# A new order of TensorE's groups and new offsets for the other engines' work, in a kernel that two long strings schedule

## The chip, the cores and the metric

The kernel runs on one core of one Trainium2 chip. The core has a matrix engine (TensorE, PE in the profile, with PEld for its weight loads), a vector engine (VectorE, DVE), an activation engine (ScalarE, ACT), GpSimd (POOL) and SyncE (SP), which here only issues DMAs. Each engine works through its own queue in order, and queues wait for each other through semaphores. The metric is the device time of one execution in microseconds, as a median of several.

## The reference, cut to what matters

Four blocks in a row, each added to a residual stream `x` of 2048 tokens by 448 features: attention with a recurrent memory, a gated feed-forward, and the same two with the same weights again.

```python
def _A_ref(x, mem0, Wq, Wk, Wv, Wo, seg_len):      # 16 heads of 256, 8 memory rows, segments of 32
    mem = mem0
    for s in range(n_seg):                          # 64 segments
        h = concat([mem, x[segment s]])             # 40 rows
        q, k, v = h @ Wq, h @ Wk, h @ Wv            # per head
        p = softmax(where(mask, q @ k.T * scale, -1e9))
        o = sum over heads of (p @ v) @ Wo
        mem = o[:8]                                 # goes into the next segment
        outs.append(o[8:])
    return concat(outs)

def _B_ref(x, W_gate, W_up, W_down):
    return (relu(x @ W_gate) * (x @ W_up)) @ W_down

x = x + _A_ref(layernorm(x), ...);  x = x + _B_ref(layernorm(x), ...)
x = x + _A_ref(layernorm(x), ...);  x = x + _B_ref(layernorm(x), ...)
```

The memory makes each attention block a chain of 64 segments that can't be worked on side by side. The token rows of a segment and the feed-forward can be done at leisure once their memory or their `x` is there.

## The kernel before, in words

**Weights.** In the first part of the run Wq, Wk, Wv and Wo come in by DMA; TensorE transposes them (L750) and multiplies them to per-head products `A` (Wq times Wk) and `Bsb` (Wv times Wo) (L763), which ScalarE and VectorE copy out of PSUM. From then on attention needs only `A` and `Bsb`.

**The chain.** `chain(step)` (from L907) does the memory rows of both attention layers together, the second seven steps behind the first (`LAG = 7`), so there are 70 steps. A step is a row of six hops between TensorE groups. U: two groups of 56 matmuls multiply the memory by `A` (L936), and VectorE turns the result in 32x32 blocks (L1107, L1114). Scores (L1130), then a softmax on VectorE and ScalarE. P: a transpose of the probabilities (L451 with `Pm`). Y: probabilities by rows (L1187, L1190), copied to `YTm`. O: 56 matmuls with `Bsb` in groups of 20, 20 and 16 (L975), split into a high and a low part by ScalarE and VectorE (L981, L982). cols: eight small matmuls (L451 with `Sel`) that turn the result into columns, copied to `mT` (L998), which the next step's U reads. In some steps more rows ride in the spare columns of these groups (the functions `ride` and `third`; tiles `Pr`, `PTr`, `Tr`).

**The rest.** `att_group` does the token rows of a tile of 128 tokens (L1276 for U, L1302 scores, L451 for the output), `glu_units` and `glu_down` the feed-forward (L1374, L1379, L1380, L451), `norm` a layer norm with its transposes. `tiles` adds these beside the chain's steps.

**The order.** Nothing is issued as it is written. Each operation is entered by `_Sched.add` with engines that may do it, a cost in ns, what it reads and writes, and a priority. `_Sched.schedule` then plays all engines against these costs and puts out one list for each engine.

- TensorE's list isn't chosen by priority. `line` (L189 on) takes the 2179 TensorE groups in the order in which the program enters them, and each letter of the string `LINE` (L46 on) says which of those that are left comes next: A is the first that is left, B the second, and so on; `~` adds 80. A group may be some few matmuls or 56.
- On the other four engines the plan takes, whenever one is free, the operation with the lowest priority among those ready. Chain operations have level 0 and go first. All else has `now`, the chain step that it belongs to, plus an offset from the string `ORDER` (L33 on): each letter is the offset of one unit of work (such as one weight load, one layer norm, one feed-forward quarter), from -6.5 to +6.5 steps in quarters. Work that either ScalarE or VectorE may do goes to the one that is free first in the plan.
- Where the plan sees TensorE idle for more than about 300 ns, `filler` puts in matmuls that compute nothing (L1408), for four fifths of the hole. A change of the tile shape of TensorE (`mode`: the whole array, 32 columns, 64 rows and so on) costs the plan `TURN = 94.0` ns.
- `emit` writes the lists out with semaphore waits, and ScalarE begins with a table load (L401).

```python
    def line(self):
        left = [o for o in self.ops if "pe" in o.engs]
        ...
            out.append(left.pop(k + SIGNS.index(c)))
    def part(self):
        self.unit += 1
        self.shift = 0.25 * (STEPS.index(ORDER[self.unit]) - 26) if self.unit < len(ORDER) else 0.0
    def add(...):
        ...
        o.prio = ((self.now if now is None else now) + (self.shift if level > 0 else 0.0), level)
```

Of the kernel before, what the change touches and what calls it, by code (L numbers as in the profile page):

```python
# [12 lines left out]
D = 448  # L13
H = 16
# [15 lines left out]


STEPS = "ABCDEFGHIJKLMNOPQRSTUVWXYZabcdefghijklmnopqrstuvwxyz0"
ORDER = ("WaAPMPvTtHAmiKXsPbQwBZAAKVLahkUWfxoglheAggVZZIjCfbeJAXlzkAApmXXSQGGARFrGGMUgYLYEqpMcimntsnbaLdDaYNUaIKQasootaa"  # L33
         "IamHzatMbanGYaAKt0aaJQPfHNWZggWPXLeJgyAiS0Lu0paxXy0bJaaawJabqAwkXQsLnJ0P0xdYLuR0IrxJESoh0aprYvAKeakBaTde0apmfl"
         "0AxKjloNZCHdAbpsDsUzAeRDrSYQfCauramiRROdJWQSliYOAntmwDkLvpaU0ose0NVHbcTnnAxX00lknAmXoAEI0JXsWoNrWtaR0aBTzbAueA"
         "zxZcQ0q0gag0TH0DuL0awknFmlrwNUBkrnZMushahJaOgAABbmsGORqpMzXeAbTAdCgmAA0qpoI0a00TKDzwtajkhAYHgKXubMoLxaAcZMeAky"
         "UPvecasMa0GlwBpnnaDqvPuaft0lUJZwIPBAtdSRexIzd0gdp0TFG0ZVaWtamLdLF0tecZgoaFmCnSxLrSAKbVEWWUbAUcbZAQKUWznAD0DwFY"
         "LhfiQS0H0vSOAAXZbJUSsFaria0uvIkcEZwBqzeVgvNgOaALCXLR0bnstXIDN0xuLBcRcqpzdacfaiZlTMhk0gMMHRwaBkgAisGZYtMsUFn0zV"
         "IFNwJApRZfcAiutYgwLmYo0w0xvGkIAceuiXs0DasLaajayO0oeyil0F0AqRaRioYDVAtQYbmvOVuSte0WMUqA0yKPaKRav0IjNTTO0lKZJvdk"
         "PxyqdoWnhLpAGweRybtOxXTBtFxgRZFGuwtA0XA0luZtjAvlcgOC0JAfaBWaBpTiUEtfuUcpuev0O0plQOMQhQAShmmAGTYotfgpbleII0TaBM"  # L40
         "aPnZY0dxoBWpVcrAiqamnnNot0unVPyLvpKpqAsABVrANdQWsSSKlz0JcSfj0ElEpn0qPKwWzaAgaYo00Aa0Tlb0oupJCA0yVSxuTnA0zokfbp"
         "CrqRqZjtboAdaHNayVAlkpQAMirRvHYYjqcposgwBwuwNAPImgFcnygdasArDIapCO00J0IZchpGLumthtqLsYG0apAkaPAtIR0rAB0uPdaaaa"
         "aacpbuKLoaaaaaaaaaaaaaaaaaaaOmqe0NbraUgWsbrP")

SIGNS = "ABCDEFGHIJKLMNOPQRSTUVWXYZabcdefghijklmnopqrstuvwxyz0123456789+-*/=<>()[]{}.,:;!"
LINE = ("AFFFEIFLJHFEFEFEJJEFGFHEEAEDMHHEDDEDEDDLKHDGDFDDDDKAJ,CEDEDCCCCKJAEGCEDBBMBBIACEBDCAAJALAHEnAADCCFGDEBAdcAWAMA"  # L46
        "AWnBAETkCSBBAHANNAgMBAKBWCAHAHGBbDAUDCAYBHBAAADPAENREAFLQHABQFPPFAFBDACCCCFBBABAAAWAAAKARBAHOdAGSAZAQAAABMS~DB"
        "A~BggA(AeCAAbAa9AZZZDADCAETADDQQAAAAMAAKKKAJJAIHAHGABEBACABAAAABATMAXAKVcLKAMRX~JXAMLA~NAAAEEADGAaaFFCCABETBBR"
        "WACPAANNNOAALAMvLA0DJCIHHLGGGGAFHHAADEKAACBBAEAAAABAMBAYXQAJGaIIAQAVAAAGDDAODDdcAFBBDDAAUaAACRAQBBNNNNAALAALL3"
        "3JKArIOICHBGGGAFIHeAEAEAACBBFAAAABCAATMBAXWeAJUaKJhMAW]AcKKAAAKEEATDA76fGmF2CABF4yBxAAAuuuCBbsAEpRFponEAAAjBLB"  # L50
        "glQAe9eeeECHcbTcbSBYBuFWBAATAARAJDSOOOAAMANLNMBdAbJDIAAPGUGZBgYBeEEEFHAGQDAvuCD~LCCqADAnNrm~BDCkkkFAAhDD;hhAAA"
        "cdjDACCYAAAVaAUATTTA0TBRDQQBBANAAAKCJBAHHHAKHGBBSGGAdcDEAZALQCBKZJBXBBBUIcJIFFBADGA))CEEon/H)CAB9jA7KD5556AA3H"
        "A32Ahzhy4FAAvAulCsssAiBEEonBFmmlDDATNCflCWABbJJEYsYYYCYXKXAWWAAITAAAAPODVNbNNNAALLEJAK+9YYDD5AA9E2FA0DIyyyzAOH"
        "vAvvBRsRBxqADACCAAjDAhDCFieeeAAcDJAaaxCCAXAAVAZAnSSssWARRRBABANAAZAACBAAGYSdlSSHGhZAFRAVAMDYABBeKBBBxHYBJEEB)("
        "HGDACOG+CA=B7ADe4CAG1112bAAyAAxxwdDkAzsbBFgoEnEmmmneFAEiENihFf-DeAGchABa2IZZZBCXAYIVXWEATDARCAAOfTBNUBMMMPBLEA"
        "L98DXeDVGIA0FAQAwFDTt~JDssstAZApArqDnANDCjAiEAmAfCCdAcccEAAZAYAAAWWAAAaTSvnARsRABBANNNAAMLAAXdAAAqBTGdASFFhPYF"
        "AQAACSBBgMBBBbIBQEBI{]ACSCC<FECCA+LEA7gD5556AA3A44bAiz70AZAxAwvluuuvAcsGHqqqGGAFtmFFFjIiBEAEeeeINEeAaAcbFBkEYA"
        "GATaAASRDHPVDOOOAANMA//ACIJA8=OOVH4Nc26BA000BAPyDwAvvNCSCAqEBAnNClCoAjjjEAiAgOC4CeeAAAbCAYBBAVqyVAAASSSASoACAA"
        "AMAAKYAdtkCJVIATISAGZgAFAAACNARMBeLdBBBFQFBADA))FCEoE/CAN>BE8B7AnCC333AGA0A21EYEexvAAVtb;rriBBArnnnCDmlQAkkPCB"
        "NAmfAAAcAaaBZZZCAYXFXHWWIAGADRXAAPANNEMMMEMVVNLEJRA77Ife4AHA16B0BAyyyAfCAuAtvuAsKAJpDAtHmAlBBKiiiEAAfAeCBddEAA"  # L60
        "DCXAWAAUZAAmStSSSASogAAAOBibxAvAZAAjYXgAJeYViYJJBnAASGAAARDC1cCJAZIBBBzIyIBEJEEBD77GFAnCIC0AB4BxB~NwAXuuu~GDtA"
        "VAtsGFADoAPsAljAjiANMfffAAdNAAdcBQYZAOBJUBLSBWRrGQQQRSDIDNDGNMLAFaJCAAGOATAEYEEEIFAACAAxwCMCTsABDBHnsAmMCBjjjA"
        "JAhCfAgfC}BAcDAAZYBXAAVVVWAATAVUsrSTAYuBRAAOOAAMMMAAKAYeAtkBWJBAIHkRbRFGSBdBEUEDOAMCCCGGCFIC{]ItU,(ADAA/BA-NB9"
        "99+AKA6CA65CdBA81bAAA3x3BwvmuuuActtsGtsHGGzpGGGmGApkjISAAfffEDdOcIeee;DaHbDYDejYfPWWeWWWXAAUNBBcbB/xQQYAdDAVDM"
        "TCARRRAACRPOKQQDGLCAAKIAAHAFFAEEEAACCABAWOVJHMARXFBAUAHAAGFAAALCCPDCDCFAJJFEBBBBBAABAADAAAAABAAAAA")


class _Op:
# [19 lines left out]
class _Sched:  # L88
# [29 lines left out]
# [5 lines that stand above are left out]
# [66 lines left out]
    def line(self):  # L189
# [3 lines left out]
        k = 0  # L193
        for c in LINE:
            if c == "~":
# [1337 lines left out]
```

## Time and profile before

| what | value |
|---|---|
| time, median of three runs | 1505.74 us (1505.22 to 1508.84) |
| time of the profiled execution | 1504.3 us |
| its span, first to last instruction | 1501.8 us |
| PE busy | 1487.6 us, 99% of the span, 37022 matmuls |
| PEld busy | 1057.6 us, 70% |
| DVE, ACT, POOL busy | 1148.6, 908.3, 171.8 us (76%, 60%, 11%) |
| granted TensorE clock | 1.000 |
| DMA | 34.11 MB; 228 and 186 GB/s in the first two of 40 slices (75 us), 4 to 65 GB/s after them |

Busy time on PE counts a matmul from its start to its modelled end. Matmuls follow each other before the one ahead has ended (a 128x448 one lasts 352 ns, and the next starts 189 ns after it), so short pauses don't show as idle. To see them one has to look at the starts: a group's time here is from its first matmul's start to the next group's first start.

### The profile page before, as it was taken

What the parts mean: (1) busy time and instruction counts of PE and PEld (TensorE: products, weight loads), DVE (VectorE), ACT (ScalarE), POOL (GpSimd) and SP (SyncE); (2) the same over time, 40 slices, a digit from 0 to 9 for tenths busy, and PEclk for the clock granted to TensorE, in tenths of its full rate; (3) what the DMA queues carried; (4) which work ended last, traced back from release to release, by engine and by line L of the source; (5) the groups of instructions that cost most, each with busy time, mean ns of one, the idle gap of its engine ahead of it and who ended that gap; (6) DMA issues with size and microseconds to landing.
All of it is one profiled execution on the core that took longest, in us unless ns stands there. A gap on an engine that the chain in (4) does not pass through costs nothing.

```text
span 1501.8 us, 83238 instructions
## 1 busy us (share of the span) xinstructions
PE 1487.6 (99%) x37022; PEld 1057.6 (70%) x37022; DVE 1148.6 (76%) x3561; ACT 908.3 (60%) x2519; POOL 171.8 (11%) x664
## 2 busy tenths in 40 slices
PE   9999999999999999999999999999999999999999
PEld 6557666667767776777768677677768776677776
DVE  6667678787778878687877877687777788787864
ACT  7776566666556666566655666466665556565643
POOL 3110111111111111011100111011100011010000
PEclk9999999999999999999999999999999999999999
DMA  7612100000000000000000000000000000000000
GB/s 228 186 31 65 50 11 8 12 9 8 8 4 16 8 8 14 4 18 6 16 5 11 12 8 15 4 17 6 18 4 8 13 9 14 5 11 5 12 8 11
DMA packets 62581, 34.11 MB, mean 23 GB/s; under 512 B 31872, under 2 KB 62096, under 8 KB 62224
## 3 DMA queue, kind: packets, MB, share of 16 engines
q1 hardware_dynamic: 62224, 28.80, 7.5%
q8 instruction: 291, 4.77, 1.3%
q14 instruction: 66, 0.54, 0.1%
HBM read 21.36 MB, written 1.84 MB: 15 GB/s over the span
## 4 chain that ended last, share of the span: by engine, by line
PE 95%; DVE 3%; ACT 1%; SPq 0%; issue 0%; DMA 0%; POOL 0%; DVEq 0%
PE psG L451 24%; PE psG L1276 17%; PE psG L1374 12%; PE psC L975 11%; PE psC L936 9%; PE psG L936 3%; PE psG L1187 3%; PE psG L763 3%; PE psG L1302 3%; PE psC L451 2%; PE psC L1187 1%; PE psC L1130 1%; PE psG L750 1%; PE psG L1190 1%; PE psC L1276 1%; PE psG L975 1%
## 5 line engine op out<-in xcount | busy, mean ns | idle before, releaser
L1276 PE MATMUL psG<-HT,A 64*128 64x128 bf16 x4968 | 285.7, 216 | 0.2
L451 PE MATMUL psG<-Bsb,YT 128*128 128x448 bf16 x1288 | 276.6, 352 | 0.0
L1276 PE MATMUL psG<-HX,A 64*128 64x128 bf16 x3726 | 266.9, 216 | 0.2 <-issue 0.2
L1276 PEld LDWEIGHTS psG<-HT,A 64*128 64x128 bf16 x4968 | 234.2, 94 | 13.7 <-issue 5.4
L441 ACT ACTIVATE Ug<-psG 64x128 bf16<-64x128 f32 (+2 forms) x428 | 153.6, 378 | 68.3 <-PE psG L1276 59.4
L1276 PEld LDWEIGHTS psG<-HX,A 64*128 64x128 bf16 x3726 | 194.0, 94 | 1.0 <-issue 0.8
L1374 PE MATMUL psG<-G,glu 64*128 64x128 bf16 x5936 | 187.9, 216 | 0.6 <-DVE G L444 0.2
L1374 PEld LDWEIGHTS psG<-G,glu 64*128 64x128 bf16 x5936 | 174.2, 94 | 12.8 <-issue 6.3
L975 PE MATMUL psC<-Bsb,YTm 128*32 128x448 bf16 x3584 | 181.4, 353 | 1.0 <-DVE YTm L444 0.6
L451 PEld LDWEIGHTS psG<-Bsb,YT 128*128 128x128 bf16 x1288 | 112.5, 97 | 89.3 <-issue 5.9
L936 PE MATMUL psC<-A,mT 64*32 64x448 bf16 x3948 | 154.7, 350 | 1.5 <-DVE Pr L1160 0.5
L1114 DVE STREAM_TRANSPOSE uT<-Usb 128x384 bf16<-128x384 bf16 x280 | 154.1, 551 | 0.9
L936 PE MATMUL psG<-A,mT 64*32 64x448 bf16 x3892 | 152.1, 350 | 0.0
L975 PEld LDWEIGHTS psC<-Bsb,YTm 128*32 128x32 bf16 x3584 | 89.9, 97 | 73.4 <-DVE YTm L444 3.1
L441 ACT ACTIVATE YT<-psG 128x448 bf16<-128x448 f32 x238 | 120.6, 543 | 11.3 <-PE psG L1190 10.4
L444 DVE CAST Ug<-psG 64x128 bf16<-64x128 f32 (+2 forms) x274 | 112.8, 422 | 18.4 <-PE psG L1276 14.6
L936 PEld LDWEIGHTS psC<-A,mT 64*32 64x32 bf16 x3948 | 79.6, 92 | 58.1 <-ACT mT L441 5.9
L1379 ACT ACTIVATE hG<-psG 128x512 bf16<-128x512 f32 (+1 forms) x126 | 68.5, 544 | 65.6 <-PE psG L1374 61.6
L451 PE MATMUL psG<-glu,hG 128*128 128x448 bf16 x448 | 98.6, 352 | 0.0
L1380 DVE TENSOR_TENSOR hG<-hG,psG 128x512 bf16<-128x512 bf16 (+1 forms) x117 | 70.7, 610 | 32.5 <-ACT hG L1379 31.5
L981 ACT ACTIVATE Ohi<-psC 128x448 bf16<-128x448 f32 x66 | 35.9, 544 | 95.5 <-PE psC L975 94.2
L936 PEld LDWEIGHTS psG<-A,mT 64*32 64x32 bf16 x3892 | 79.8, 92 | 17.3 <-ACT mT L441 0.6
(242 smaller groups left out, 2889.4 us busy)
## 6 DMA issues: line engine op xcount, KB each, us to landing
HR<-xn SPq DMA_DIRECT2D x128, 32.0 KB
Tsb<-Rsb SPq DMA_DIRECT2D x256, 1.5 KB
Tsb<-Rsb SPq DMA_DIRECT2D x256, 2.0 KB
Bsb<-in_A_Wq_dram SPq DMA_DIRECT2D x6, 384.0 KB
Bsb<-in_A_Wk_dram SPq DMA_DIRECT2D x6, 384.0 KB
HR<-Rsb SPq DMA_DIRECT2D x126, 1.5 KB
HR<-Rsb SPq DMA_DIRECT2D x126, 2.0 KB
X<-in_A_x_dram SPq DMA_DIRECT2D x16, 112.0 KB
```

The costliest lines, as they stand in the source:

```text
L441: return E.activation(out, i, ACT.Copy, scale=1.0 if scale is None else scale)
L444: return E.tensor_copy(out, i)
L451: return E.matmul(out, lhsT=lhsT, rhs=rhs, **k)
L763: i = E.matmul(bk.ap()[row0:row0 + mn, 0:D], lhsT=lhs[:, et, m0:m0 + mn], rhs=rhs[:, et, :], start=(et == 0), stop=(et == 1), tile_positio ...
L936: i = E.matmul(ub[v].ap()[32 * j:32 * j + 32, 0:D], lhsT=self.mT[rw, WHERE[b], first:first + 32], rhs=cols, start=(b == 0), stop=(b == 6), ...
L975: x = E.matmul(bo.ap()[32 * j:32 * j + 32, 0:D], lhsT=self.YTm[:, q, :], rhs=self.Bsb[:, chunks[q], :], start=(i == 0), stop=(i == 13), ti ...
L1114: self.s.add("dve", 578, lambda E, e, out=out, hh=hh: E.transpose(out, heads[hh]), r=[("Usb", 2 * half + v) for v in range(2)], w=[f"uT{ha ...
L1187: return E.matmul(ps[:, n * q:n * q + n], lhsT=HR[rows, 128 * q:128 * q + 128], rhs=PT, start=True, stop=True, tile_position=(b, 0))
L1276: i = E.matmul(ub[v].ap()[:, 128 * n:128 * n + 128], lhsT=self.A[rw, b, a0:a0 + 128], rhs=HT[rw, WHOLE[b], :, 0:SEG] if CROSS[b] is None e ...
L1374: i_ = E.matmul(two[v].ap()[:, 128 * c:128 * c + 128], lhsT=self.Wgu[rw, b, f0:f0 + 128], rhs=G[rw, WHOLE[b] if CROSS[b] is None else 4 + ...
L1379: s.add("act", 170 + 0.833 * N, lambda E, e, dst=dst, z=two[0], N=N: E.activation(dst, z.ap()[:, 0:N], ACT.Relu), r=[two[0]], w=[("hG", i, ...
L1380: s.add("dve", dv_cost(N), lambda E, e, z=two[1], N=N, dst=dst: E.tensor_tensor(dst, dst, z.ap()[:, 0:N], ALU.mult), r=[two[1]], w=[("hG", ...
```

## The change

Only two strings change, `ORDER` and `LINE`; both keep their lengths (1144 and 2188 letters). No cost, no operation, no buffer and no line of the scheduler changes. 918 of the 1144 offsets differ, by 3.7 steps in the mean over all units. TensorE's list holds the same 2179 groups: 1711 of them stand at another place, half of the 2179 by at most two places, a tenth by nine or more. Which of ScalarE and VectorE does a copy, the order of the four other queues (SP's DMA issues too) and the place and length of the fillers follow from the two strings through the plan.

```diff
-ORDER = ("WaAPMPvTtHAmiKXsPbQwBZAAKVLahkUWfxoglheAggVZZIjCfbeJAXlzkAApmXXSQGGARFrGGMUgYLYEqpMcimntsnbaLdDaYNUaIKQasootaa"
+ORDER = ("XVAPMPSPU0eQshNDJHlyQAAKEKFYTTnKhsVEoiWWUsPWZFARZjHv0fMpppVAINWUUAOrD0QTKksvPJgInbSAlblsqlxarfpaoAOa0ePaAklvaa"
...
-LINE = ("AFFFEIFLJHFEFEFEJJEFGFHEEAEDMHHEDDEDEDDLKHDGDFDDDDKAJ,CEDEDCCCCKJAEGCEDBBMBBIACEBDCAAJALAHEnAADCCFGDEBAdcAWAMA"
+LINE = ("AFEEEEIIEGFEFEADLDJDHGEEEDADCKIDDEDDECDCJJDHCABBCBCBI:JHBDBBBBCBI/HEDBFBCBCBKJHEEBBBBCJMQAIALHBABBCBAACBcbCDQA"
...
```

More of the change, by code (lines that the diff above doesn't have):

```diff
@@ L32 @@
 STEPS = "ABCDEFGHIJKLMNOPQRSTUVWXYZabcdefghijklmnopqrstuvwxyz0"
-ORDER = ("WaAPMPvTtHAmiKXsPbQwBZAAKVLahkUWfxoglheAggVZZIjCfbeJAXlzkAApmXXSQGGARFrGGMUgYLYEqpMcimntsnbaLdDaYNUaIKQasootaa"
[L34 to L43, printed above, removed]
@@ L45 @@
-SIGNS = "ABCDEFGHIJKLMNOPQRSTUVWXYZabcdefghijklmnopqrstuvwxyz0123456789+-*/=<>()[]{}.,:;!"
-LINE = ("AFFFEIFLJHFEFEFEJJEFGFHEEAEDMHHEDDEDEDDLKHDGDFDDDDKAJ,CEDEDCCCCKJAEGCEDBBMBBIACEBDCAAJALAHEnAADCCFGDEBAdcAWAMA"
[L47 to L65, printed above, removed]
@@ new lines @@
+ORDER = ("XVAPMPSPU0eQshNDJHlyQAAKEKFYTTnKhsVEoiWWUsPWZFARZjHv0fMpppVAINWUUAOrD0QTKksvPJgInbSAlblsqlxarfpaoAOa0ePaAklvaa"
+         "kaDeOadS0aKAVafat0aazKWAaNyNXfiPeVuAGylprp0uru0wsw0E0aaaGRaxybEaX0yGIn0XoMgxLwXAAcxczAOvYaEEAqASAawYaubP0apdBA"
+         "sTxVVYRNZUv0niphIsAAAexRNc0AEDanFaSSG0adAY0VWivQtAcmy0EgWp0VoIpAuNHdofTutDcgsHlQoqXfoPSQhoXVUTrEuvaboax0AKKuVn"
+         "WAncs0R0QajonAPDvHgUaAhFSLLWZUUFFdAaPGfaDNaXX0NvbFhG0iqIAqLJAlfFKXgpPcDQhkY0gmJvKgs0eAjeceOkAGAuuQvEAaVwaUJASC"
+         "moqJ0aFJaQnWiSpJynhYv0sAe00KopJkIyFurlwneQIvUVgNiFsVyPlCaLBa0nmAn0cszQVohYYJdSNCBgWKfMARARUZULd0OQCstQyAAPAPGd"
+         "kzfmqu0n0EuOViX0EvncHIaGna0fxVAc0JqxgzwNZeagVksirXHIGpAjMXFVAC0ucDpHYjs0naAwaUgBoIhILJLYH0lwAsgw0uoVYqAiGGRvOV"
+         "tsczJPYIAtcumpA000AmO0oomxGtOtmcMtXQNkAaAaauXfFS0HVf0e0rMAUXaTUj0AVjfQR000OAJua00LqkwckmjJabRaA0iHrTyIRYaZYbDC"
+         "dxAmVLdndMkAN0ADyh0HAXApAiOg0onIXR0s0AOiCIZBuAgDcCrEijEJafxagtPenEAAKbdpUXIqt0ReMAvQrmZxqYsAVWknQfjIM0kVPkbaAi"
+         "aArgBmdD0EUlVDXociaEYhTQtrwpaLMPjpHjtEsjpRdtNeUA00QuczhBsRJjjfobBnogkgx0faNeaMNuVkaAaQREoCXUHF0fviaYTDHwHGuYbA"
+         "OcRdqSykHAZVaCdaVIGhqpAdHEtRmWRNMqmAc0JwpLstiGnRmPLPAymSaZorejTAgj00VhynXhSyEcEtsLKYDJiQaXOTaqy0WB0S00fPLuaaaa"
+         "aawW0IKgJaaaaaaaaaaaaaaaaaaaJtaktN0AagUYWbrA")
@@ new lines @@
+SIGNS = "ABCDEFGHIJKLMNOPQRSTUVWXYZabcdefghijklmnopqrstuvwxyz0123456789+-*/=<>()[]{}.,:;!"
+LINE = ("AFEEEEIIEGFEFEADLDJDHGEEEDADCKIDDEDDECDCJJDHCABBCBCBI:JHBDBBBBCBI/HEDBFBCBCBKJHEEBBBBCJMQAIALHBABBCBAACBcbCDQA"
+        "BFDUAOjAAQAPDeANNAgMBAKBAAHbICGBDAZCCLAAHAVAGXAADOADMCCADPJFAHOENNEHFEBACGBBBABAAAWAAAKARBAHOdHASAZAQAAAUNB~DB"
+        "A~BggA(DACcAAaADY7EDWWWGAATADDRQAAAAMAAKKKAJJAIAIHABFAADACBAAAABAMSZhAAKVLbKASM~JXALLA~NAAAEEAHDAGFYYCHCCUABBX"
+        "RACPAANNNAALAKMvLA0KCPJIICHHHAGIIAAEFAADCCBAEAAABABAMAAXXHAOIaASIAWGAAAGDDAOACCcbBEBADCAbADSAAQAPBAMMMMAAKALL3"
+        "3LJQAqJIIBHHHAGAIHeAAFDAACBBFAAAABCAAMSBAXWeKAUaJiJAXLdAsLKAAAEEIATDAC65ElEHCAzBBx2AweDCtttGAAqAsrDPDAAmkBLBin"
+        "QAffVeeeBUDcHZZZCYYwHBFAUAAAREJADrNhDMMMNAAKAYLDIKJZIgfDHAAFTKFeFFFbBTAGDACuuD~MCCAqBPDBmAl~BCBjjjEjAAgDC:hgFd"
+        "AAbEDZAAAWbAAUAXTTTAASyAQCQPAANAAAKPAAIAHHHKAGBTBGGdAVACACLBVKKbNBRiBLVLBBBRFFBEAAF[)Gqp<CCA)*NA+MB888EKAA4A65"
+        "BjBA1zAZ4DAAvuctCjrrrArhHEFXlFmlAD7jpACYCfLCdcDbbbCJZbZAAYYBFAUUAAAAQACT5OcCCMMMPNAKKAK98ZYJ5DAAU1ABzKAxxxAxIC"
+        "uTDSCssABoAouCAlCBjADIgEDAdddAAbACbbyDCXAXAAAUAYSvSlsARRRACAAAMAAKYADjAiIaUAAlHGRhQAYFAQAACYBBfeLLBBBFKFBAUDA>"
+        ">oGFC*CCCADB6ACd3BA5111FaAAxAzynDctAtbiIBTotFnmEEkkkVkbEEgADDeeL9GDJaAiAYdXXqXXXBJVAWWoIAbUSAACQAAdCNqMSMMMPFM"
+        "rAAJAH33VUCCzAAE2PvACtTCCqqqAQBDnmAnmD]CjAiADAfCCdAgEbbbAAZAABAXXAUAAaTSvnARsRABBANNNOAALAYeAAiBqIUBAHGQiaQAFA"
+        "APACSBBgBBBJIaBEBOI]]ACCC>AQBCC(-BEA8hD666AA4A55AbA2EA6AzxXxdvdAtttICrAFrrEADmunPDDDDinQgFkfDEJcccAAaCZaZFBhXB"
+        "BAETAXDHQHDUOOOAAMA==DKAKIA8POHA4AL2R111AAPzyACyyCTCSuLFqxAApOnn~AEDlllAlAAiQDAhgD2CdAcEAgAZDCXAAAAASSSTAoSDBd"
+        "AANAAAAWjAiIUZDAGGRAAOeEAAANBRhBLVLBBBFFBEHMAA))FRFo=CCCAE9=LA7oDD444AAF1AEz10EgxYwAAAcVxriq}ApppADDmAQmmCCPjC"
+        "CCmgABcdJCCZBYYYCCXHVAVWVHAJRAAAOGTAALbLRLLLVLNKKR98AffJ4A9CkA0BByADwwwAAuuAvuBKAqJpAAnHBAk>AAiiiJDAgAeAAAddDA"
+        "ZDCXAAVAATASuSSSAShoAAAPBBMBZfvACjXABWVAdHTTaBBSGFAQZPiENWNAMNDLABBVtIBBBFnQBEGBD87EoEmAeCCAyBBDv0eAt~JDCrrr~D"
+        "VqqAgqpHnETSAjAoADgBfBeeeBBBcbMREaZCXBWObAFTFZFRGAEOOOAGAMLALLKcFaAPIAAOUGAAEXEEEAACCBCAwvCLBSAZpAICAlqBkLBiii"
+        "AJDAeAdfeC{BbAaACAXBBVAYUUUAASATTqqRARuQCPAOAAMMMAMAKAAXdtCBIUogUJIAbRFBYFRcBBDCOCALBBBFKAEADA))sGS<CAB*AB+M99"
+        "9A9DKA5A76CdBk9A1ADxAYwA01uultttAcsHqqGrqHoGfGlrAFFipFBgHfffAFedJOuecddDDI{YZDDDWbVEUdUUUACVLRAXQaZw-QEXAAVNZD"
+        "TMOCQQQFAAQNADCPOAJAAKIAAHFAEEADDDUEACAQBAITAbAZAFXJENJDHAABHADDAPCCACBLADACCAAAAAAAAADAAABABAAAAA")
```

## The prediction

> **What bounds the kernel.** I read the page's first parts, then TensorE's waits, then stretches of time, then the timeline of one stretch.
>
> ```profile
> PE 1487.6 (99%) x37022; PEld 1057.6 (70%) x37022; DVE 1148.6 (76%) x3561; ACT 908.3 (60%) x2519; POOL 171.8 (11%) x664
> ```
> ```profile
> 0.00:53.20 53.20, 50.45 (x575) 32.84 (x575) 36.38 (x82) 40.73 (x65) 13.75 (x44) 1.00 0.85 248
> 53.20:314.40 261.20, 254.45 (x6053) 167.70 (x6058) 189.50 (x575) 164.90 (x439) 30.83 (x118) 1.00 0.13 35
> 314.40:1416.50 1102.10, 1100.50 (x28533) 797.86 (x28531) 871.02 (x2766) 664.29 (x1919) 124.63 (x493) 1.00 0.05 10
> ```
>
> The second view gives, for a stretch, the busy time of PE, PEld, DVE, ACT and POOL, the clock, DMA share and GB/s. TensorE is the bound everywhere, at full clock, and the same matmuls run after the change. So the question is what TensorE spends on anything else. Busy time hides it (fillers count as busy, and so do pauses under the length of a matmul); the starts show it. Here are chain step 6 and the start of step 7 on PE (start, length, line, count):
>
> ```profile
> 162.66 1.52 PE L936 MATMUL psC<-A,mT 64*32 64x448 bf16 x56
> 163.99 1.51 PE L936 MATMUL psG<-A,mT 64*32 64x448 bf16 x56
> 165.43 1.74 PE L1374 MATMUL psG<-G,glu 64*128 64x128 bf16 x56
> ...
> 171.21 0.55 PE L451 MATMUL psG<-glu,hG 128*128 128x448 bf16 x2
> 171.91 2.83 PE L975 MATMUL psC<-Bsb,YTm 128*32 128x448 bf16 x56
> 174.68 0.40 PE L451 MATMUL psG<-ident,xn 128*128 128x128 bf16 x4
> 174.91 0.92 PE L1408 MATMUL psG<-A 128*128 128x448 bf16 x4
> 176.40 0.19 PE L451 MATMUL psC<-Sel,Ohi 128*128 128x32 bf16 x1 [0.56 <-DVE Olo L984]
> ...
> 176.61 0.35 PE L1408 MATMUL psG<-A 128*128 128x448 bf16 x1
> 177.35 0.97 PE L1302 MATMUL psG<-HT,Ug 128*128 128x40 bf16 x32 [0.40 <-POOL HT L1008]
> 178.25 1.52 PE L936 MATMUL psC<-A,mT 64*32 64x448 bf16 x56
> ```
>
> Two things are to be seen. From U's first half to its second, 1.33 us; from the second to a group with another tile shape, 1.44: a **change of shape** costs about 0.1. And from O's end to cols, and from cols to the next U, the chain goes through other engines; too little work stands there, and TensorE runs **fillers** (L1408) and waits. I took every group from start to start, with the median of groups that precede one of the same shape as the group's own time, and 94 ns (847 against 753 ns ahead of another shape, 4 matmuls of L451; 1657 against 1563, 56 of L1374) for a change. The sum over the 2179 groups:
>
> - own time of the groups: 1408.2 us, which no order changes
> - 610 changes of shape: 57.3 us
> - fillers, 51 matmuls with the pauses around them: 13.0 us
> - all other pauses: 18.6 us, of them 12.4 in 55 pauses over 60 ns
> - start, last group and last addition and store: the rest of 1501.8.
>
> The 31.6 us of fillers and pauses lie as follows: 6.2 ahead of chain step 0 (53.2 us), where weights still land; 17.6 in steps 0 to 14 (to 314 us); 7.9 in the 54 steps to 1416 us. This is all that an order can win, plus what it saves in changes.
>
> **The change part by part.**
>
> *Changes of shape.* I took the letters of both `LINE` strings one by one, as `line` does, and counted neighbours with different shapes: 617 before (fillers in between make it 610 in the trace), 598 after. 19 fewer times 94 ns: **-1.8 us**, on TensorE itself, so hidden by nothing. [...] The row shows less than a full drain (352 ns of a 128x448 matmul less the 189 between two starts are 163 ns); at 163 the term would be -3.1.
>
> *The holes of the chain, steps 0 to 14.* For each step I compared its six hops: the time that a hop took in the trace, and the TensorE work that stands inside it in either order (own times and changes). The shortest time that a hop took in any of the 70 steps: U to scores 2.68, scores to P 1.70, P to Y 0.49, Y to O 0.85, O to cols 1.70, cols to U 0.81 us. Where less work than this stands in a hop, TensorE must pause. Summed over steps 0 to 14, old against new: U to scores 1.03 and 1.34; scores to P 0.49 and 0.43; P to Y 1.48 and 1.46; Y to O 1.59 and 0.90; O to cols 4.31 and 4.25; cols to U 1.67 and 0.98. Together 10.6 and 9.4: **-1.2 us**. In step 6 above, Y to O gets 0.79 us of work in place of 0.57 and cols to U 3.35 in place of 0.90, but O to cols keeps its 0.32, which is where most is lost. If a hop that paused needs again what it took in the trace, it is 14.9 and 13.9: -0.9. I take -1.2. The two agree since the big holes stay: in steps 5, 6, 10 and 14 the same hops stand as empty as before.
>
> *Steps 15 on.* By the shortest hops 0.2 us of holes before and 0.0 after; by what paused hops took, 5.0 and 7.5 (U to scores 2.4 and 6.2, the other five together 2.5 and 1.3). So -0.2 to +2.5; I take **-0.2**, since 54 of the 70 U hops didn't pause at all. The 7.9 us of pauses here are thus hardly holes of the chain; they are chance: an operation late in the queue of ACT or DVE, or a PSUM bank not yet free. Counting banks in use from a group's start to its copy's end, with the median time of each copy, a ninth of eight is wanted 3 times after 300 us in the old order and 8 in the new; over all groups seven or eight are in use 266 and 260 times. That speaks neither way.
>
> *The start.* The first 16 loads on SP keep their order (priority 0); offsets move the later ones. The trace has the first weights of the second group landed at 14.4 us and their transposes at 19.2; the new order wants them 4 us of work earlier, so it waits there, but has no more work behind than before: the loads that it needs next land at 18.0 and 19.6, and the old order stood at the same two. Step 0 begins after 47.1 us of work before and 47.7 after, which moves work and removes none. One load of x goes ahead of weights on SP, 0.6 us of issue. I take 0, with -1 to +1.
>
> *The offsets.* No instruction is added or removed on ACT, DVE, POOL or SP. Most operations hide behind TensorE work (DVE is busy 76%, ACT 60%). If the cover goes, each late copy is a pause of 0.1 to 0.6 us, as the 55 were. Bounds for all of these together: the chance pauses fall by a third of 15 us (25.6 from step 0 on less the 10.6 that the shortest hops force), -5, or a U hop slows, below. Middle: 0. The first table load (1.28 us on ACT from 0.73, in the row of L401) comes before any ACT copy; the cost list that makes the queues has no term for it before or after, and TensorE's warm-up runs to 6.73 us beside it. Worth 0.
>
> Sum against the profiled execution: 1504.3 - 1.8 - 1.2 - 0.2 = **1501.1**. That execution lies 1.4 below the median of the runs, so the median comes to **1502.5**.
>
> **The rivals.**
>
> *Forecast, 0.40*: as above; by itself 1500 to 1505.
>
> *More falls, 0.27*: the chance pauses go too. For it: holes and chance pauses are of one size, and a third of 15 us is only some 20 of the 55. Against it: nothing that I can count in the new order speaks of it. 1501.1 - 5 = 1496.1, median 1497.5.
>
> *Less, or it isn't what it says, 0.16*: the table load is no hole, the chain's gain (1.2) is used up by new chance pauses, and only shapes count. 1504.3 - 1.8 + 1 = 1503.5, median 1505.
>
> *Slower, 0.17*: the U hop. Behind U, two copies, three turns on DVE of up to 0.55 us and a POOL or ACT copy must go through queues whose order is new. If the hop takes 3.2 us (a quarter took at most that), steps with less work in it than needed: 23 before, 27 after, short by 6.8 and 8.7 us; at 3.65 (the median of those that paused), 44 and 47, short by 21.7 and 25.9. The old hops paused 6.4 in all. It decides from 9.6 us on (6.4 and the 3.2 gained), at about 3.25 us a hop. Halfway between 8.7 and 25.9, 17.3, it costs 10.9: 1512.0, median 1513.4. For it: DVE is the second busiest engine, and the new order puts less work in this very hop. Against: most old hops lived with as little.
>
> **How the numbers follow.** A measurement of this kernel can tell about 0.3% (4.5 us) from no change: faster is under 1501.2, slower over 1510.3. The forecast lies a little above the first bound, and a third of it falls below: faster 0.40 x 0.32 + 0.27 x 0.95 = 0.39; slower 0.17 from the last case and 0.01 from the third; the rest, 0.43, within. The range goes from 1495 (the second case with -1 at the start and 163 ns for a change of shape) to 1510 (the slow case with a few of its hops); what lies out of it is most of the slow case and a little of the second.
>
> **What would show it.** Right: 11 to 27 fewer changes of shape at about 94 ns; the fillers of L1408 still near 40 to 50 matmuls, with the hole from O to cols in steps 6, 10 and 14; stretches after 314 us as long as now, within 3 us. Wrong: a chain step after 314 us with U to scores over its work by 0.5 us again and again (the slow case); fillers under half of 51, or the pauses after 314 us under 4 us (the second). What would make it wrong altogether is a load that lands later because SP's queue changed: PE's waits would name a DMA in the first 70 us.

## The result and the profile after

| what | before | after |
|---|---|---|
| time, median of five runs, same comparison | 1505.22 us (1504.62 to 1508.84) | 1500.58 us (1499.25 to 1502.11) |
| time of the profiled execution | 1504.3 us | 1501.67 us |
| its span | 1501.8 us | 1499.8 us |
| matmuls on PE | 37022 | 37018 |
| fillers (L1408), matmuls | 51 | 47 |

The ratio is 0.9967, 95% interval 0.9957 to 0.9978: 4.6 us less by the medians and 0.33% by the ratio, with an interval that lies on both sides of the 0.3% that the prediction drew as its line. The forecast was 1502.5 us.

The first lines of the page of the changed kernel, busy time of each engine:

```profile
span 1499.8 us, 83215 instructions
...
PE 1484.8 (99%) x37018; PEld 1057.2 (70%) x37018; DVE 1135.5 (76%) x3526; ACT 918.9 (61%) x2554; POOL 170.5 (11%) x664
```

Some 35 operations went from DVE to ACT, which follows from the new strings through the plan. TensorE is 99% busy, as before. Two stretches, steps 0 to 14 and steps 15 to 68 of the changed kernel (PE, PEld, DVE, ACT, POOL, clock, DMA share, GB/s), and then steps 15 to 68 of the kernel before (the prediction's third stretch ends one step earlier):

```profile
53.90:313.10 259.20, 253.25 (x6048) 166.85 (x6051) 186.49 (x566) 164.73 (x447) 31.17 (x120) 1.00 0.13 36
313.10:1432.70 1119.60, 1117.23 (x28976) 810.91 (x28978) 873.95 (x2778) 684.12 (x1974) 123.88 (x494) 1.00 0.05 10
```
```profile
314.40:1433.20 1118.80, 1117.20 (x28921) 808.82 (x28920) 882.42 (x2801) 673.46 (x1944) 125.46 (x496) 1.00 0.05 10
```

Steps 0 to 14 take 259.2 us where they took 261.2, with the same DMA share; steps 15 to 68 take 1119.6 where they took 1118.8. Step 6 and the start of step 7, on PE (start, length, line, count):

```profile
165.50 1.74 PE L1374 MATMUL psG<-G,glu 64*128 64x128 bf16 x56
...
171.87 2.83 PE L975 MATMUL psC<-Bsb,YTm 128*32 128x448 bf16 x56
174.63 0.36 PE L1408 MATMUL psG<-A 128*128 128x448 bf16 x1
175.28 0.40 PE L451 MATMUL psG<-ident,xn 128*128 128x128 bf16 x4 [0.28 <-POOL xn L1216]
175.51 0.54 PE L1408 MATMUL psG<-A 128*128 128x448 bf16 x2
176.22 0.19 PE L451 MATMUL psC<-Sel,Ohi 128*128 128x32 bf16 x1 [0.17 <-DVE Olo L984]
...
176.44 0.35 PE L1408 MATMUL psG<-A 128*128 128x448 bf16 x1
177.18 0.97 PE L1302 MATMUL psG<-HT,Ug 128*128 128x40 bf16 x32 [0.39 <-POOL HT L1008]
...
180.53 1.52 PE L936 MATMUL psC<-A,mT 64*32 64x448 bf16 x56
```

The hole from O (L975) to cols (L451 with `Sel`) stands where it stood and is as empty as before: four matmuls of a transpose, which now come 0.6 us later within it, and three fillers. The hop took 1.70 us, the shortest time that the prediction lists for it. Behind cols, the group of L1302 waits 0.39 us for the copy of `HT`, as it did (0.40). U now comes 2.4 us of L1276 later than that group (at 180.53 us) instead of right behind it, but the pause stands ahead of L1302, where the added work fills nothing.

The account from start to start, made as in the prediction, for both kernels and for a second profiled execution of each (taken with the experiments; "idle" is fillers and pauses, in us):

| kernel | shape changes | start | steps 0 to 14 | steps 15 on | all idle | span |
|---|---|---|---|---|---|---|
| before | 610, 57.3 us | 5.4 | 17.8 | 7.9 | 31.6 | 1501.8 |
| before, again | 610 | 6.0 | 20.0 | 7.7 | 33.7 | 1503.9 |
| after | 592, 55.7 us | 5.4 | 15.9 | 9.7 | 31.3 | 1499.8 |
| after, again | 592 | 5.9 | 15.5 | 8.0 | 29.5 | 1498.0 |

(For the first row the prediction has 6.2 us for the start and 17.6 for steps 0 to 14; counted again they are 5.4 and 17.8.) The two profiled executions of one kernel differ by 2 us, as much as the terms that are sought. By the means of the two: 1.7 us less for changes of shape, 3.2 us less in steps 0 to 14, nothing at the start, and 1.1 us more in steps 15 on.

### The profile page after: what moved, and what is told of

It is laid out like the page before. It is cut to its first block, busy times and chain, and to the rows that moved or that the text cites. A ratio compares the mean times of both kernels' runs of the same rounds, so it can differ in the third digit from the quotient of the medians.

```text
span 1499.8 us, 83215 instructions
## 1 busy us (share of the span) xinstructions
PE 1484.8 (99%) x37018; PEld 1057.2 (70%) x37018; DVE 1135.5 (76%) x3526; ACT 918.9 (61%) x2554; POOL 170.5 (11%) x664
## 3 DMA queue, kind: packets, MB, share of 16 engines
q8 instruction: 291, 4.77, 1.4%
## 4 chain that ended last, share of the span: by engine, by line
PE 95%; DVE 2%; ACT 1%; SPq 1%; DMA 1%; issue 0%; POOL 0%; DVEq 0%
PE psG L451 25%; PE psG L1276 17%; PE psC L975 12%; PE psG L1374 12%; PE psC L936 9%; PE psG L936 4%; PE psG L1187 3%; PE psG L1302 3%; PE psG L763 3%; PE psC L451 2%; PE psC L1130 2%; PE psC L1187 1%; PE psG L750 1%; PE psG L1190 1%; SPq L711 1%
## 5 line engine op out<-in xcount | busy, mean ns | idle before, releaser
L1276 PE MATMUL psG<-HT,A 64*128 64x128 bf16 x5020 | 290.2, 216 | 0.0
L451 PE MATMUL psG<-Bsb,YT 128*128 128x448 bf16 x1344 | 286.7, 352 | 0.0
L1276 PE MATMUL psG<-HX,A 64*128 64x128 bf16 x3765 | 270.3, 216 | 1.6 <-issue 1.6
L1276 PEld LDWEIGHTS psG<-HT,A 64*128 64x128 bf16 x5020 | 238.0, 94 | 11.7 <-issue 4.1
L1276 PEld LDWEIGHTS psG<-HX,A 64*128 64x128 bf16 x3765 | 197.4, 94 | 2.4 <-issue 2.2
L441 ACT ACTIVATE Ug<-psG 64x128 bf16<-64x128 f32 (+2 forms) x446 | 161.2, 378 | 59.2 <-PE psG L1276 49.4
L975 PE MATMUL psC<-Bsb,YTm 128*32 128x448 bf16 x3696 | 187.1, 353 | 0.3
L451 PEld LDWEIGHTS psG<-Bsb,YT 128*128 128x128 bf16 x1344 | 117.8, 97 | 98.7 <-issue 9.7
L936 PE MATMUL psG<-A,mT 64*32 64x448 bf16 x4088 | 159.3, 350 | 0.0
L975 PEld LDWEIGHTS psC<-Bsb,YTm 128*32 128x32 bf16 x3696 | 92.7, 97 | 72.4 <-ACT YTm L441 1.0
L444 DVE CAST Ug<-psG 64x128 bf16<-64x128 f32 (+2 forms) x266 | 109.9, 421 | 17.3 <-PE psG L1276 12.7
L451 PE MATMUL psG<-glu,hG 128*128 128x448 bf16 x448 | 98.2, 352 | 0.2 <-DVE hG L1380 0.2
L936 PEld LDWEIGHTS psG<-A,mT 64*32 64x32 bf16 x4088 | 83.5, 93 | 18.4 <-ACT mC L441 0.5
L982 DVE TENSOR_TENSOR Olo<-psC,Ohi 128x448 bf16<-128x448 f32 x68 | 42.3, 622 | 67.4 <-ACT Ohi L981 66.8
```

The lines of the kernel that those rows point to most:

```text
L441: return E.activation(out, i, ACT.Copy, scale=1.0 if scale is None else scale)
L444: return E.tensor_copy(out, i)
L451: return E.matmul(out, lhsT=lhsT, rhs=rhs, **k)
L936: i = E.matmul(ub[v].ap()[32 * j:32 * j + 32, 0:D], lhsT=self.mT[rw, WHERE[b], first:first + 32], rhs=cols, start=(b == 0), stop=(b == 6), ...
L975: x = E.matmul(bo.ap()[32 * j:32 * j + 32, 0:D], lhsT=self.YTm[:, q, :], rhs=self.Bsb[:, chunks[q], :], start=(i == 0), stop=(i == 13), ti ...
L1276: i = E.matmul(ub[v].ap()[:, 128 * n:128 * n + 128], lhsT=self.A[rw, b, a0:a0 + 128], rhs=HT[rw, WHOLE[b], :, 0:SEG] if CROSS[b] is None e ...
```

## The experiments

All kernels compute all of the reference. Each was compared with the kernel before on the same chip; medians of the kernel before were 1502.7 to 1505.5 us over the chips, so ratios are to be compared.

**The changed kernel once more, and the kernel before once more.** No edit.

> The changed kernel once more, unchanged, to see how far one execution differs from another. The two profiles at hand differ by 2.0 us of span (1501.8 and 1499.8), the medians by 4.6. Theory A (the order saves shape changes and holes, and the rest is which executions were profiled): median 1499 to 1502 again, 592 shape changes at 94 ns again, and a profile whose idle time (31.3 us of fillers and pauses) moves by 1 to 2 us with no change in the order, mostly in the start. Theory B (the change is worth the whole 4.6 and the profiled execution was an odd one): this profile's span lies near 1497, with the missing 2.5 us in the pauses of steps 15 to 68.

Measured: 1499.48 us against 1503.24, ratio 0.9970 (0.9957 to 0.9982). The trace has 592 changes again and 1.8 us less idle time, as theory A had it, but what moved is steps 15 on (9.7 to 8.0 us) and not the start; its span, 1498.0, lies between the two theories.

> The kernel before, once more, for a second profile of it. Theory A (the order's part is 610 changes of shape, holes of 17.8 us in steps 0 to 14 and some 8 us of pauses in steps 15 to 68; one execution differs from another by 1 to 2 us in the pauses): span 1499 to 1502, steps 0 to 14 at 17.8 give or take 0.3, and 2.4 to 2.5 us of the execution's time outside the span, where the changed order has 1.8 to 1.9. Theory B (the first profile of it was an odd one): pauses in steps 15 to 68 over 9.5 us or a start over 7.

Measured: 1504.84 against 1505.48, ratio 0.9994 (0.9985 to 1.0003). Its span is 1503.9 and the time around it 1.8 us, where the first profile of before had 2.5; so the time around the span doesn't belong to the order, as theory A had thought. Steps 0 to 14 had 20.0 us idle where theory A had 17.8 give or take 0.3; 2.7 of it are pauses in the midst of groups, which the last run is about (0.7 in the first execution). The same two stretches in the second profiles, before and then after:

```profile
53.80:317.00 263.20, 255.20 (x6045) 168.16 (x6046) 189.44 (x574) 165.03 (x439) 30.77 (x118) 1.00 0.13 35
317.00:1435.60 1118.60, 1117.04 (x28928) 808.61 (x28925) 881.69 (x2801) 673.42 (x1944) 125.09 (x496) 1.00 0.05 10
```
```profile
54.50:313.20 258.70, 253.19 (x6048) 166.86 (x6051) 186.66 (x566) 164.66 (x446) 31.15 (x120) 1.00 0.13 34
313.20:1431.00 1117.80, 1115.86 (x28968) 810.65 (x28966) 873.46 (x2777) 683.06 (x1974) 123.92 (x494) 1.00 0.05 10
```

Steps 0 to 14 of one kernel took 261.2 and 263.2 us, of the other 259.2 and 258.7: the gain there stands in both pairs. Steps 15 on took 1119.6 and 1117.8 in two executions of the same instructions.

**One string without the other.** Which of the two strings carries the gain?

```diff
 e1: the changed kernel with the old offsets
-ORDER = ("XVAPMPSPU0eQsh...
+ORDER = ("WaAPMPvTtHAmiK...
 e2: the changed kernel with the old order of groups
-LINE = ("AFEEEEIIEGFEFE...
+LINE = ("AFFFEIFLJHFEFEF...
```

> The new order of TensorE's groups with the old offsets for the other engines. Theory A (the group order itself carries the gain through fewer shape changes and fuller chain hops, the offsets only have to keep out of the way): shape changes 592 give or take 10, -1.7 us by that term; holes of steps 0 to 14 near 16 us; and if the old offsets serve the new order as well, 1501 to 1504. Theory C (the two strings are one plan, and each is worth something only with the other): operations stand late in the queues of ACT and DVE, pauses in steps 15 to 68 go from 9.7 us to 15 to 30, and the time is 1508 to 1525.

> The old order of TensorE's groups with the new offsets. Theory A: shape changes back at 610, no gain from them, 1504 to 1508. Theory C: pauses in steps 15 to 68 from 7.9 to 15 to 35 us, time 1512 to 1530. Theory D (the gain sits in the offsets, by which the other engines come earlier): 1500 to 1503 with the old group order.

Measured: 1513.9, ratio 1.0068 (1.0055 to 1.0082), and 1520.26, ratio 1.0115 (1.0101 to 1.0129). Each half alone loses; the gain belongs to neither. Where the new order has the old offsets, the loss is mostly in the start (13.5 us idle, 11.5 in steps 15 on, where theory C had looked for 15 to 30). Its timeline on PE:

```profile
30.02 1.51 PE L750 MATMUL psG<-ident,Bsb 128*128 128x128 bf16 x24
31.37 8.98 PE L1408 MATMUL psC<-ident 128*128 128x128 bf16 x158
40.33 0.40 PE L451 MATMUL psG<-ident,xn 128*128 128x128 bf16 x4
```

One filler of 158 matmuls bridges 9 us until a layer norm's transposes. The new order wants the second tile of `x` there, and by the old offsets its load is issued at 33.4 us (33.0 in the trace of before, where it landed at 37.3; 20.6 in the changed kernel). In the other mix steps 15 on have 22.2 us idle, 13 of them fillers, so holes that the plan itself saw. The two strings are one plan, which is what theory C said, and the theory that the offsets alone carry the gain (D) falls.

**No fillers.**

```diff
-                room = [(t, b) for b, (t, _) in empty.items() if t is not None and t <= free[e]] if n > 0 else ()
+                room = ()
```

> The changed kernel without the fillers that the plan puts into holes (the 17 matmuls at the very start stay); they compute nothing. If the holes are the chain's and the loads' own latencies, as the prediction counted them, the 47 filler matmuls cost nothing and their 11.9 us turn into plain pauses: time within 1.5 us of the changed kernel's 1500.6, granted clock still 1.0. If fillers lengthen holes (a matmul of 350 ns still running when the chain's next group is ready, and the two shape changes around it): 2 to 5 us faster. If the clock needs them: granted clock under 1.0 in the first 100 us and 2 us or more slower.

Measured: 1500.29 (1498.37 to 1503.74), ratio 0.9982 (0.9974 to 0.9991), beside 1499.48 and 0.9970 for the changed kernel on the same chip: 0.8 us more by the medians and 1.8 by the ratios, with intervals that overlap. The single executions tell more. In three of the eleven the mean granted clock was 1.000, and they took 1498.4, 1498.6 and 1500.3 us, about what the changed kernel takes; in three it was 0.997, and they took 1503.0, 1503.0 and 1503.7. So fillers save some 4 us where the clock falls to 0.997 without them (1503.0 to 1503.7 against 1499.48) and nothing where it stays at 1.000, and no cost of theirs shows. The profiled execution is one of the slower three. Three stretches of it (columns as above):

```profile
172.50:175.90 3.40, 3.40 (x58) 1.82 (x59) 2.18 (x5) 1.02 (x2) 0.00 (x0) 1.00 0.02 5
175.90:179.30 3.40, 1.68 (x37) 0.84 (x26) 2.77 (x10) 2.88 (x7) 0.76 (x3) 1.00 0.08 22
179.30:182.70 3.40, 3.40 (x78) 3.35 (x78) 2.26 (x12) 1.14 (x5) 1.01 (x4) 0.50 0.09 24
```

After a stretch in which PE was busy 1.68 of 3.40 us, at the hole of step 6, the granted clock was 0.50 for the next 3.4 us. It happened once more, after the hole of step 14 (2.07 of 3.40 us busy, then 0.51 from 315.8 to 319.3 us). In the kernel with the new order and the old offsets a stretch of 1.73 of 3.40 us was followed by a clock of 1.00:

```profile
138.90:142.30 3.40, 1.73 (x55) 1.53 (x52) 1.71 (x6) 1.56 (x5) 0.29 (x1) 1.00 0.23 63
142.30:145.70 3.40, 3.40 (x35) 1.73 (x35) 2.47 (x7) 1.64 (x5) 0.00 (x0) 1.00 0.20 58
```

**The first table load in the plan.** ScalarE's own list gets a first entry of the 1283 ns that the row of L401 shows.

```diff
         free = {e: 0.0 for e in self.ENGS}
+        free["act"] = 1283.0
```

> The changed kernel with the first table load as 1283 ns of ScalarE's time ahead of everything in the plan that makes the queues, which the change itself doesn't have. The prediction priced the table load at nothing, since no ScalarE result is wanted before 6.7 us: the time stays within 1 us of the changed kernel's, the start's idle time at 5.4 to 5.9 us. If the plan's first queues are wrong for want of it: the start's idle time falls by 0.5 us or more, and one or two copies go from ACT to DVE in the first 3 us.

Measured: 1499.22 against 1503.52, ratio 0.9970 (0.9961 to 0.9979), the start 6.0 us idle against 5.4 and 5.9: the same as the changed kernel. The table load is worth nothing that shows, as the prediction had it. TensorE's list in this kernel is that of the changed kernel, group by group, so its profile counts as a third execution of that list below.

**More changes of shape.** 24 pairs of neighbouring groups are swapped in `LINE`, far from the chain's holes, so that 48 more changes stand in the list. One of the swaps:

```diff
-...YYwHBFAUAAAREJADrNhDMM...FTKFeFFFbBTAGDACuuD...
+...YYwHBFAUAAAREJADrNhDMM...FTKFeFFFbUBAGDACuuD...
```

> The changed kernel with 24 pairs of neighbouring groups of steps 15 to 68 swapped where two groups of one shape stand before two of another, so that each swap adds two changes of shape: 48 more, the same work. At 94 ns each (the prediction): 640 changes in the trace, +4.5 us, 1504 to 1505 beside a changed kernel of 1499.5 to 1500.6. If a change drains TensorE in full (163 ns): +7.8. If a change is hidden behind other waits in steps that pause anyway: under +2.

Measured: 1503.59, ratio 1.0000 (0.9991 to 1.0008), against 1499.22 for the kernel with the table load on the same chip: 4.4 us for 48, 91 ns each. In the trace 640 changes cost 60.2 us, 94 each. A full drain (the author's estimate of 163 ns from the profile's modelled ends, 352 ns of a 128x448 matmul less the 189 between two starts; 7.8 us in all) doesn't fit. What TensorE does in the 91 to 94 ns isn't shown.

**The new order in one half of the run.** The first 470 groups and 239 units from the new strings and the rest from the old ones, and the other way round.

```diff
 first half new: the line of ORDER with unit 239
-         "sTxVVYRNZUv0niphIsAAAexRNc0AEDanFaSSG0adAY0VWivQtAcmy0EgWp0VoIpAuNHdofTutDcgsHlQoqXfoPSQhoXVUTrEuvaboax0AKKuVn"
+         "sTxVVYRNZUv0niphIsAAAexDNc0AEDauraSSRROdAYQSliYOAntmwDkLvpaU0ose0NVHbcTnnAxX00lknAmXoAEI0JXsWoNrWtaR0aBTzbAueA"
...
 second half new: the same line
-         "sTxVVYRNZUv0niphIsAAAexRNc0AEDanFaSSG0adAY0VWivQtAcmy0EgWp0VoIpAuNHdofTutDcgsHlQoqXfoPSQhoXVUTrEuvaboax0AKKuVn"
+         "0AxKjloNZCHdAbpsDsUzAeRRrSYQfCanFamiG0adJW0VWivQtAcmy0EgWp0VoIpAuNHdofTutDcgsHlQoqXfoPSQhoXVUTrEuvaboax0AKKuVn"
...
```

> The new group order and offsets up to the middle of chain step 14 (the first 470 groups, which are the same set in both orders, and the 239 units of work that they belong to), the old ones after that. Theory A (gain = fuller hops in steps 0 to 14, plus fewer shape changes after them): idle time of steps 0 to 14 near 15.7 us (before: 17.8), steps 15 to 68 near 8 as before, 13 more shape changes than the changed kernel has in all beyond its own saving, so about 616; span 2.1 less and 0.6 more for shapes: 1.5 us under the kernel before. Theory E (the gain is all after step 14): same as before or up to 1 us slower.

> The other half: old order and offsets up to the same point in step 14, new ones after it. Theory A: about 24 fewer shape changes in steps 15 to 68 (-2.3 us), idle time there 8 to 10 us against 7.9, start and steps 0 to 14 as before (5.4 and 17.8): 0.4 to 2.3 us under the kernel before. Theory E: the whole gain, 4.6 under.

Measured: 1502.98, ratio 0.9999 (0.9990 to 1.0008), and 1500.86, ratio 0.9983 (0.9974 to 0.9992). The counts explain why the first half gains so little by itself: its 617 changes of shape are 7 more than before (+0.7), and the second half's 585 are 25 fewer (-2.4). In the first kernel's trace steps 0 to 14 have 16.6 us idle, 1.6 of it one pause in the midst of a group; in the second 17.9, as before, and 7.1 in the start. So the traces show the holes filled by the first half and the shapes saved by the second. By the time the second is -2.6 where its shapes say -2.4, but the first is only -0.5 (-1.5 to +1.2 by the interval) where its terms say -1.7. The two together gain 3.2 us, and the whole change on this chip 4.3 (the kernel with the table load); where the rest went isn't shown.

**Less work in the hop from U to scores.** In ten of the steps from 18 to 62, groups are moved out of this hop until 1.3 to 2.0 us of work is left in it; it is the slower rival's mechanism made on purpose.

```diff
-...HZZZCYYwHBFAUAAAREJADrNhDMM...
+...HZZZCYYwHXBFAAAAREJADrNhDMM...
```

> The changed kernel with the hop from U to scores thinned out in ten steps from 18 to 62: groups that stood inside it are put right behind the scores, so that 1.3 to 2.0 us of work is left where 2.8 to 4.5 stood. 18 more changes of shape (1.7 us). Theory A (a hop needs its shortest time, 2.68 us, and what is missing is a pause): 9.1 us of new pauses, 10.8 in all, 1510 to 1511 beside a changed kernel near 1499.8. Slower rival of the prediction (a hop needs 3.65 us, the median of the hops that paused): 18.7 us, 20.4 in all, 1519 to 1521. If U's results could come earlier still than any hop showed (2.4 us): 6.3, 8.0 in all, about 1508.

Measured: 1511.75 against 1505.48, ratio 1.0039 (1.0026 to 1.0051): 0.72% over the changed kernel's ratio, 10.8 us. The ten hops took 2.68 to 3.26 us, 2.91 in the mean, with 1.78 of work inside in the mean; that is 11.2 us, and 18 more changes of shape 1.7, together 12.9. The idle time of all steps 15 on rose by less, from 8.0 and 9.7 us to 18.8, so some pauses that stood there before are gone. A hop that is short of work needs 2.7 to 3.3 us, 2.9 in the mean: more than the shortest time, so that the 10.8 us of theory A came out exactly is in part luck. The rival's 3.65 was too much.

**A plan that is meant to be robust.** Both strings searched further, with the other engines' costs also at 3% more, so that fewer pauses should come from an operation that is a little late.

```diff
-ORDER = ("XVAPMPSPU0eQsh...
+ORDER = ("YSxMMamJn0Gfdw...
-LINE = ("AFEEEEIIEGFEFE...
+LINE = ("AFENFEIJIEAGEE...
```

> Two new strings, found from the changed kernel's by small moves that were kept when they lowered the mean of two planned spans: one with the plan's costs, and one with every cost of ACT, DVE, POOL and SP 3% higher. 608 changes of shape in place of 598. In the plan it is 1.3 us longer than the changed kernel with the plan's costs, and 8.5 shorter with the higher ones. Theory A (the pauses of steps 15 to 68 are small delays that the plan doesn't see, so an order that stands them better pauses less): 0.9 us more for shapes, 3 to 5 us fewer pauses, 1496 to 1498. If only the nominal plan counts: 1 to 2 us slower, 1501.

Measured: 1503.0 (1499.12 to 1505.07), ratio 0.9983 (0.9973 to 0.9993), 2.4 us slower than the changed kernel by the ratios. Steps 15 on had 10.2 us idle, 3.7 of it in the midst of groups, where no other engine's work is waited for; that led to the last run. Theory A's 3 to 5 us fewer pauses didn't come. This speaks against small delays as the main cause of the pauses there, but one order that was made with 3% higher costs doesn't rule them out.

**Where the instructions lie.** Some pauses stand in the midst of a group, between two matmuls of the same kind with the same inputs ready. In the timeline of the changed kernel on PE:

```profile
536.34 0.34 PE L1187 MATMUL psG<-PTx,HR 40*128 40x128 bf16 x6
536.51 0.22 PE L1190 MATMUL psG<-PTx,HR 40*128 40x64 bf16 x3
537.26 0.19 PE L1190 MATMUL psG<-PTx,HR 40*128 40x64 bf16 x1 [0.53 <-issue]
537.27 0.34 PE L1374 MATMUL psG<-G,glu 64*128 64x128 bf16 x5
```

The fourth matmul of L1190 comes 0.53 us late, and the profile names no releaser. PE's waits after 313 us say the same for the larger of them (us, times, longest):

```profile
PE psG L1276 <- issue: 1.0, 3, 0.4
PE psG L1190 <- issue: 0.7, 2, 0.5
PE psC L451 <- DVE Olo L984: 0.2, 1, 0.2
PE psG L1302 <- issue: 0.2, 1, 0.2
```

And the table of DMA queues on the page:

```profile
q8 instruction: 291, 4.77, 1.4%
```

291 packets with 4.77 MB are 16 KB each. If PE's 74 thousand matmuls, weight loads and waits are what they hold, that is some 64 bytes an instruction and 256 instructions a packet, an estimate from these counts. Theory F: TensorE now and then gets to the end of what is loaded before the next packet is there. If so, moving all of its instructions by some places within the packets must move the pauses, with the same plan and the same data. The warm-up, 17 matmuls ahead of any input, is cut differently, which puts 112 instructions more ahead of all others:

```diff
-            for _ in range(17):
+            for _ in range(64):
+                i = E.matmul(wb.ap()[:, 0:32], lhsT=hG[:, 0:128], rhs=hG[:, 128:160], start=True, stop=True)
+            for _ in range(9):
```

> The changed kernel with another warm-up ahead of everything: 9 of its 17 matmuls of 448 columns and 64 of 32 columns, so that all of TensorE's later instructions stand 112 places further on in its instruction stream, in the same order and with the same plan. Pauses in the midst of a group (no wait stands there) end 1.2 to 1.7 us after a 16 KB load of instructions has ended, in ten profiles so far; in the changed kernel's two profiles four of them recur at the same groups, at 378.8, 513, 536 and 688 us. Theory F (TensorE runs out of instructions where groups with many short matmuls stand together at the end of a block of 16 KB, which holds 256 instructions): with the blocks' bounds moved by near half a block, at least three of the four are gone, others stand elsewhere, their sum is again 2 to 4 us, and the time stays within 1.5 us of the changed kernel's. Rival (the pause belongs to these groups: a bank, a copy, a clash of reads): the four stay where they are.

Measured: 1498.7 (1496.97 to 1500.75), ratio 0.9973 (0.9963 to 0.9983). The four pauses in the midst of groups that came back in both executions of the changed kernel (at 378.8, 513, 536 and 688 us) are all gone; others stand elsewhere, 7 of 0.2 us or more with 2.4 us together. By itself this shows little: in the kernel with the table load, the third execution of the unmoved list, only the one at 536 us came back. Two counts over more pauses are stronger. In the three executions of the unmoved list, 13 places have a pause of 0.1 us or more in at least two of them, and the moved list pauses at none of the 13. And over 13 profiled executions all 99 pauses of 0.2 us or more in the midst of groups end 1.2 to 1.7 us after a 16 KB packet has landed; in the changed kernel only a tenth of the time lies in that range. Both are as theory F has them, and the rival, that the data or the PSUM banks at these places make them, falls. The time is that of the changed kernel within the intervals.

## Why the prediction was off by a little

- **Changes of shape, -1.8**: right. 18 fewer in place of 19, at 94 ns in the traces and 91 by the time of 48 more: -1.7. No run shows the 163 ns that the prediction's range has at its low end; the runs showed these 94 and 91.
- **The holes of steps 0 to 14, -1.2**: right in kind, too small in size; this is the term that was mis-sized. Without the pauses in the midst of groups (of 0.2 us or more) the whole stretch went from 17.1 and 17.3 us to 14.7 and 14.8, about -2.4. The pauses in the six hops alone fell by 1.9 us: counted like this they are 14.7 and 15.1 in the two executions of before, 12.9 and 13.0 in those of after, and the half-and-half kernels agree (13.0 with the new order up to step 14, 14.7 with the old one). Hop by hop, U to scores fell by 0.4, where the shortest times had it rise by 0.3; Y to O fell by 0.9 (0.7 said), O to cols by 0.4 (0.1 said), and cols to U by 0.4 (0.7 said: step 6 shows why, a group within the hop waits for the same copy as before). The rest, some 0.5, lies outside of the six hops, where the prediction had no term. One of its floors wasn't one: the hop from U to scores, 2.68 us at the least, took 2.59 and 2.37 in step 9 of the changed kernel. The other floors stand.
- **Steps 15 on, -0.2, bounds to +2.5**: held within its bounds. +1.8 and +0.1 us in the two executions, of which pauses in the midst of groups are 3.8 and 3.0 us after, against 2.1 and 1.1 before. Without these it is some -0.7.
- **The start, 0 with -1 to +1**: right (5.4 and 6.0 before, 5.4 and 5.9 after). The sign that was to show the whole forecast wrong, a DMA among PE's waits in the first 70 us, was badly chosen: such waits are 0.2 and 0.9 us before, 1.2 and 0.9 after, and the first of after stands at 15 us, where the prediction itself had the new order wait.
- **The offsets, middle 0**: the value held, the reason didn't. The prediction put the chance pauses down to late operations on ACT or DVE and to PSUM banks, and counted banks for it. At least a part, 4 to 5 of some 30 us in the changed kernel, is pauses in the midst of groups, which end 1.2 to 1.7 us after a packet of instructions has landed; of what is left, no cause was shown.
- **The table load, 0**: right, by the run with it in the plan.
- **The sum.** For the profiled execution 1501.1 was said and 1501.67 came (1499.9 the second time). The 1.4 us that was put on top of it, for where the profiled execution lay below the median, was chance: the second profile of before took 1505.68. Of the 4.6 us by the medians, the terms above account for some 4 (1.7 and 2.4), and the rest is less than two executions of one kernel differ by. The same list gained 3.8, 4.3 and 4.0 us in the later comparisons (unchanged, with the table load, with the other warm-up).
- **The rivals.** "More falls" needed 5 us of chance pauses to go, and fillers under half of 51: 47 stand, and steps 15 on have no fewer pauses. "Less" needed the chain's gain to be used up, which one execution did (9.7 us in steps 15 on) and another didn't. The slower one is ruled out: all U hops together pause 8.5 and 7.5 us in the new order (6.4 and 7.0 in the old one), under the 9.6 from which it would have decided, and the shortened ones needed 2.9 us a hop in the mean, under 3.25.

So "within 0.3%" was thought the likeliest, and the result stands on the bound: a forecast of -3.2 us where -4.6 was measured (-3.3 to -6.5 by the interval), the larger part of the difference being the chain's holes (-1.2 said, -2.4 found).

## What to carry to other kernels

Where an engine is 99% busy, account for it from start to start, and by what the starts can't explain: here 57 us of changes of shape, 31 us of fillers and pauses. Profile a kernel twice before a term under 2 us is believed, and set a floor by the shortest of many cases only where the cases have repeated it. An order and the offsets that feed it are one plan: either without the other cost 11 and 17 us here. And a scheduler that plays the engines has a forecast of its own, which the prediction didn't use: the end of the plan (`self.span` in `schedule`) is 1488.6 us before and 1483.0 after, -5.6 where -4.6 was measured; over the changed kernel it is +17.5 and +24.9 for the two mixes, +4.5 for the added changes and +13.5 for the shortened hops, where +14.4, +20.8, +4.4 and +10.8 were measured.

## What the runs showed of the hardware that was not expected

- **Pauses in the midst of groups end just after a packet of instructions.** In each of 13 profiled executions 4 to 12 pauses of 0.2 us or more, about 2 to 5 us together, stand in the midst of groups. Each of them ended 1.2 to 1.7 us after a packet of 16 KB on the queue of instructions had landed (the kernel without fillers, where pauses at half clock look alike, is left out). Such a packet takes 1.1 us in the median and 2.4 at most in the changed kernel, 1.0 and 1.8 in the kernel before. In the changed kernel one comes every 5.2 us in the mean (291 in 1499.8 us), but 128 matmuls of L1276 with their weight loads, a packet by the estimate above, last only 3.6 (28 ns from start to start). That TensorE waits for the packet is inferred from these lags and from the moved list; why some packets come late and others not wasn't found.
- **Half the clock was granted after two stretches that were partly idle.** 3.4 us with TensorE busy 1.68 us were followed by 3.4 us at a granted clock of 0.50, and 3.4 us with 2.07 us busy by 3.5 us at 0.51, both in the kernel without fillers. Busy time alone doesn't decide: 1.73 of 3.40 us busy, in the kernel with the new order and the old offsets, was followed by a clock of 1.00. What does decide isn't shown.
- **Executions of one kernel differ in their pauses**, not in their work: 31.6 and 33.7 us idle before, 31.3 and 29.5 after, with the same instructions.
